# A mixed-heads attention and feed-forward kernel: second batch in float32, sums over partitions in two steps, the reciprocal behind the next maximum

## The chip, the core and the metric

The kernel runs on one core of one Trainium2 chip. The metric is the device time of one execution in microseconds (us); lower is better. The core has five engines that run their own instruction streams in order: PE (matrix products into PSUM), DVE (vector work), ACT (activation functions, copies with a scale), POOL (vector work on SBUF only) and SP, which issues nearly all transfers.

## What is computed

Two stages, joined by a reshape. Four batches, 12 heads, 448 positions, 64 features per head; then 1792 tokens of width 768 through a gated layer of width 2048.

```python
scale = 1.0 / np.sqrt(q.shape[-1])
scores = scale * np.matmul(q, k.transpose(0, 1, 3, 2))
scores = np.einsum('bhij,hg->bgij', scores, w_pre)      # mix the heads
scores = scores - np.max(scores, axis=-1, keepdims=True)
attn = np.exp(scores)
attn = attn / (np.sum(attn, axis=-1, keepdims=True) + 1e-09)
attn = np.einsum('bhij,hg->bgij', attn, w_post)         # mix the heads again
attn_out = np.matmul(attn, v)
...
h = x @ w_in                                            # x: attn_out as (1792, 768)
g = h * (1.0 / (1.0 + np.exp(-1.702 * h)))
out = g @ w_out
```

The mixing over heads is why a row of scores cannot stay inside one head: the kernel writes raw scores to DRAM (`sd`) and gathers them again with heads on partitions.

## The kernel before, in words

**Steps.** A batch's 448 query rows are cut in groups of 10 (45 groups, the last of 8). One group is one step of the main loop; `steps` lists all 180, so steps 0 to 44 are batch 0, 45 to 89 batch 1 and so on. With 12 heads a group fills 120 partitions.

In the loop turn i the code writes out, for the group i or its neighbours: `gather` for step i+4 (DMA of `r`), `mix(i+1)` on PE (the first head mixing, tile `mx`, two PSUM banks), then `peak(i)` on DVE (row maximum `nm`, read from `mx`), `expo(i)` on ACT (exponential `e` with its row sum `sm`) and, at its end, a short POOL instruction (`rs`, sum plus 1e-9). `inverse(i)` (line 304, a DVE reciprocal of `rs`) is the last thing of turn i. The next thing on DVE is `peak(i+1)`.

**Batch 0 is in float32.** `weigh_mix` (POOL) multiplies the small mixing matrix `wp` by the reciprocal, giving `wr`; `post_whole` (PE) forms the second mixing with four float32 products into `pp`, two turns after the group's own; `keep_whole` (ACT) copies `pp` to `p`. The context product (`context`, tile `av`) uses v and p in float32, and the scale that x gets is one number per batch (`xs`).

**Batches 1 to 3 split every operand in two float16 numbers.** `weigh` (POOL, `w` = e times `rs`), `upper` (ACT, `a1`) and `lower` (POOL, `a2` = w minus a1) split the weights; `post` (PE) does 12 float16 products per group, three turns after the group's own; `keep_upper` (ACT) and `keep_lower` (DVE, line 383) split the result. v is loaded twice, once for its size (`va`) and once to be split (`vb`, `vp`). q and k of batch 1 are float32 already before the change; those of batches 2 and 3 are split.

**Jobs.** The splitting of the two weight matrices (16 slices, `convert`), the loading and splitting of q, k and v, and the scales are jobs: each has an earliest turn, an engine, a cost and the jobs that it must follow. `run_jobs` is called once a turn, behind `peak` and `expo`, and starts what is due as long as its engine has tokens (4.3 a turn while nothing of the feed-forward runs, 5.2 after; jobs marked urgent don't ask). A slice of weights takes three parts: DVE decodes each with five instructions, ACT sums squares, then a sum over partitions and a scale follow, ACT writes the upper halves, DVE the lower halves (line 537), and SP stores them (`wd`).

**Sums over partitions.** `add_all` (lines 104 to 109) does such a sum in one job: a PE product with a matrix of ones into the last 16 columns of the newest `pp` bank, and directly behind it a DVE reduce of that product. There are 28 of them. DVE, which runs in order, stands at the reduce until PE has come to the product.

**The feed-forward part** is 384 quanta of six products each (`hidden`, 192, and `project`, 192). They begin when the x of a batch is complete; the loop then puts 2.15 quanta a turn behind the attention work. The first stands in turn 58. Behind the head mixing of step 179 PE still has 786 of these products left.

Of the kernel before, what the change touches and what calls it, by code (L numbers as in the profile page):

```python
# [19 lines left out]
B, H, S, D = 4, 12, 448, 64  # L20
DM, DFF = 768, 2048
# [17 lines left out]
def attention_then_feed_forward(ctx, tc, q, k, v, w_pre, w_post, w_in, w_out, out):  # L39
# [30 lines left out]
    wp = flow.tile([KG, H, GI], F32, name="wp", tag="th", bufs=2)  # L70
# [33 lines left out]
    def add_all(m, parts):  # L104
# [37 lines left out]
    def join(name, b):  # L142
        add_all(top_of(name, b), st["m" + name, b])

    def scale(name, b):
# [9 lines left out]
        if name == "v":  # L155
            nc.vector.tensor_scalar(
                ex[:, b:b + 1], e, e_wp, 2.0 ** -12, op0=ALU.mult, op1=ALU.mult
            )
            if b == 0:
                xs = st["xs"] = keep.tile([128, 1], F32, name="xs")  # L160
                nc.vector.reciprocal(xs, ex[:, 0:1])
# [61 lines left out]
    def scores(b, c, pr, tag=("gen", 3)):  # L223
# [5 lines left out]
        if b < 2:  # L229
# [59 lines left out]
    def expo(i):  # L289
# [6 lines left out]
        )  # L296
        rs = stat.tile([KG, 1], F32, name=f"rs_{i}", tag="rs")
        by = 2.0 ** -10 if steps[i][0] else 1.0
        nc.gpsimd.tensor_scalar(rs[:K], sm[:K], 1e-9, by, op0=ALU.add, op1=ALU.mult)  # L299
        row["e", i], row["rs", i] = e, rs  # L300
# [61 lines left out]
    def mixed_to(i):  # L362
# [3 lines left out]
        if off == 0:  # L366
            shape, kind = ([CP, NR, H, CI], F32) if b == 0 else ([CP, 2, NR, H, CI], F16)
            st["p", b, c] = mixed.tile(shape, kind, name=f"p_{b}_{c}", tag="p")
        p = st["p", b, c]
        if b == 0:  # L370
# [15 lines left out]
    def context(b, c, pr):  # L386
# [6 lines left out]
        if b == 0:  # L393
            for jc in range(NR):
                for d in range(2):
# [3 lines left out]
                        st["v", 0, h // w][:, h % w, jc * D:(jc + 1) * D],  # L399
                        st["p", 0, c][:, jc, h, :n],  # L400
# [21 lines left out]
    def x_upper(b, c, half, av):  # L422
        i0, n = chunk(b, c)
        by = st["xs"] if b == 0 else 2.0 ** -15
        nc.scalar.activation(x_of(b)[:, 0, 3 * half:3 * half + 3, i0:i0 + n], av, AF.Copy, scale=by)

    def x_lower(b, c, half, av):
        i0, n = chunk(b, c)
        x = x_of(b)[:, :, 3 * half:3 * half + 3, i0:i0 + n]
        by = st["xs"] if b == 0 else 2.0 ** -15  # L430
# [8 lines left out]

    def join_x(b):  # L440
        e = gs[:, b, 0:1]
        add_all(e, st["mx", b])
# [21 lines left out]
    def convert(kind, s, first):  # L464
# [46 lines left out]
        def join_w():  # L511
            t["n"] = stat.tile([128, 1], F32, name=f"{nm}_n", tag="wn")
            add_all(t["n"], t["m"])
# [45 lines left out]
        j = job(first, "D", 0.2, join_w, after=[(x, 1) for x in sizes])  # L559
# [173 lines left out]
    for b in range(1, B):  # L733
        z = GPB * b
        sizes = {}
        if b == 1:
            for i in range(THIRDS):
                for name in "kq":
                    job(z - 23 + 4 * i, None, 0, lambda name=name, i=i: load_whole(name, 1, i), urgent=True)
        for name, first, ready in (("k", z - 25, z - 17), ("q", z - 23, z - 17), ("v", z - 8, z + LAG + 7)):  # L740
            if b == 1 and name != "v":
                continue
# [6 lines left out]
            jn = job(0, "D", 0.2, lambda name=name, b=b: join(name, b), after=[(x, 1) for x in sq], urgent=True)  # L749
            sizes[name] = job(0, "D", 0.7, lambda name=name, b=b: scale(name, b), after=[jn], urgent=True)  # L750
# [6 lines left out]
        if b > 1:  # L757
            job(0, "D", 0.4, lambda b=b: mixing(b), after=[sizes["k"], sizes["q"]], urgent=True)
# [140 lines left out]
    j = job(1, "D", 0.2, lambda: join("v", 0), after=sq, urgent=True)  # L899
    job(1, "D", 0.9, lambda: scale("v", 0), after=[j], urgent=True)  # L900
# [51 lines left out]
    while quanta or i < N + LAG + 12:  # L952
# [15 lines left out]
        if GPB <= i - LAG - 1 < N:  # L968
            keep_upper(i - LAG - 1)
            spend("A", 0.55)  # L970
        if 0 <= i - 1 < GPB:
# [9 lines left out]
        if i < N:  # L981
            peak(i)
            spend("D", 0.62)
            expo(i)
            spend("A", 0.82)
# [7 lines left out]
        if GPB <= i - LAG < N:  # L993
# [6 lines left out]
        for b, c, pr in at_context.pop(i, []):  # L1000
# [7 lines left out]
            if c == NCH - 1 and pr == NPAIR - 1:  # L1008
                z = i
                a = job(z + 2, "D", 0.2, lambda b=b: join_x(b), urgent=True)  # L1010
# [4 lines left out]
                job(z + 3, "D", 0.9, finish, after=[a], urgent=True)  # L1015
# [4 lines left out]
        if GPB <= i - LAG - 1 < N:  # L1020
# [50 lines left out]
```

## Time and profile before

| | us |
|---|---|
| median of 3 runs (lowest, highest) | 1026.39 (1025.78, 1027.22) |
| the profiled execution | 1027.42 |
| its span, first to last instruction | 1025.7 |
| PE busy | 925.0 (90%) |
| DVE busy | 628.8 (61%) |
| ACT busy | 605.2 (59%) |
| POOL busy | 354.5 (35%) |
| mean granted PE clock | 0.961 |
| moved by DMA | 198.19 MB, 193 GB/s over the span |

PE is the busiest engine, but not evenly: its share is lower and its clock is below full speed in the first 45% of the span, and close to full afterwards. The transfers are the other way round: the busiest tenths of the DMA line are in the first fifth of the span. The views used below are the busy time by stage (a stage runs from the maximum of one step to that of another), the waits by stage, the groups of instructions, and the order of time for a few short stretches.

### The profile page before, as it was taken

What the parts mean: (1) busy time and instruction counts of PE and PEld (TensorE: products, weight loads), DVE (VectorE), ACT (ScalarE), POOL (GpSimd) and SP (SyncE); (2) the same over time, 40 slices, a digit from 0 to 9 for tenths busy, and PEclk for the clock granted to TensorE, in tenths of its full rate; (3) what the DMA queues carried; (4) which work ended last, traced back from release to release, by engine and by line L of the source; (5) the groups of instructions that cost most, each with busy time, mean ns of one, the idle gap of its engine ahead of it and who ended that gap; (6) DMA issues with size and microseconds to landing.
All of it is one profiled execution on the core that took longest, in us unless ns stands there. A gap on an engine that the chain in (4) does not pass through costs nothing.

```text
span 1025.7 us, 19868 instructions
## 1 busy us (share of the span) xinstructions
PE 925.0 (90%) x7344; PEld 542.4 (53%) x7344; DVE 628.8 (61%) x1389; ACT 605.2 (59%) x1380; POOL 354.5 (35%) x536
## 2 busy tenths in 40 slices
PE   5678878877899889999899999999899999999998
PEld 4345555544455444555455555656455666555554
DVE  5658786698976796554644575555645565443334
ACT  3666768677577676765657657656656564323332
POOL 0111111145433455343533454334534444001221
PEclk9888999888999998999999999999999999999999
DMA  8988979768557656654676647546654341234322
GB/s 301 289 275 313 332 267 323 259 197 245 190 198 244 232 187 181 192 172 131 202 225 207 202 150 234 166 130 179 212 164 146 108 148 64 93 123 151 118 93 85
DMA packets 66565, 198.19 MB, mean 193 GB/s; under 512 B 7668, under 2 KB 32372, under 8 KB 66468
## 3 DMA queue, kind: packets, MB, share of 16 engines
q1 hardware_dynamic: 66064, 196.83, 59.4%
q8 instruction: 58, 0.95, 0.4%
q14 instruction: 39, 0.32, 0.1%
q10 hardware_dynamic: 404, 0.09, 0.1%
HBM read 140.27 MB, written 56.62 MB: 192 GB/s over the span
## 4 chain that ended last, share of the span: by engine, by line
PE 62%; DVE 17%; ACT 8%; DMA 8%; issue 3%; POOL 1%; SPq 0%; ACTq 0%; DVEq 0%; POOLq 0%
PE po L627 19%; PE h L588 18%; PE mx L279 8%; PE av L408 4%; PE qk L243 3%; PE pp L356 2%; PE pp L358 2%; PE pp L357 2%; DVE w_p L537 2%; DMA sd<-sc 2%; ACT waste L96 2%; DVE w_f L504 2%; DMA w<-in_moe_w_out_dram 2%; DVE nm L286 2%; ACT e L293 1%
## 5 line engine op out<-in xcount | busy, mean ns | idle before, releaser
L627 PE MATMUL po<-g,wt 128*128 128x448 f16 x1152 | 243.8, 355 | 11.3 <-DVE th L609 6.8
L588 PE MATMUL h<-x,wt 128*128 128x448 f16 x1152 | 244.1, 356 | 3.9 <-ACT sc L253 2.9
L279 PE MATMUL mx<-r,wa 120*120 120x448 f32 x360 | 183.3, 592 | 40.0 <-ACT e L293 29.7
L343 POOL TENSOR_TENSOR a<-w,a 120x448 f16<-120x448 f32 x135 | 150.8, 1117 | 130.2 <-issue 71.5
L627 PEld LDWEIGHTS <-wt 128*128 128x128 f16 x1152 | 109.4, 99 | 130.0 <-issue 45.1
L588 PEld LDWEIGHTS <-wt 128*128 128x128 f16 x1152 | 109.2, 98 | 117.0 <-issue 31.2
L329 POOL TENSOR_SCALAR w<-e,rs 120x448 f32<-120x448 f32 x135 | 88.2, 653 | 227.3 <-DVE rs L304 217.8
L337 ACT ACTIVATE a<-e,rs 120x448 f16<-120x448 f32 x135 | 91.0, 674 | 106.1 <-DVE rs L304 106.1
L657 DVE SCALAR_TENSOR_TENSOR acc<-po,ct,acc 128x448 f32<-128x448 f32 x141 | 96.1, 682 | 74.3 <-PE po L627 72.2
L293 ACT ACTIVATE e<-mx,nm 120x448 f32<-120x448 f32 x180 | 113.6, 631 | 31.2 <-POOL wr L309 25.4
L609 DVE SCALAR_TENSOR_TENSOR th<-th,h 128x448 f32<-128x448 f32 x64 | 39.7, 620 | 137.8 <-ACT th L606 137.8
L606 ACT ACTIVATE th<-h,ct 128x448 f32<-128x448 f32 x64 | 40.5, 633 | 140.2 <-PE h L588 129.6
L253 ACT COPY sc<-qk 120x448 f32<-120x448 f32 (+1 forms) x186 | 89.6, 532 | 41.8 <-PE qk L233 28.9
L286 DVE TENSOR_REDUCE nm<-mx 120x1 f32<-120x448 f32 x180 | 108.9, 605 | 1.9 <-PE mx L279 1.9
L356 PE MATMUL pp<-wp,a 120*112 120x120 f16 x540 | 95.7, 220 | 14.8 <-DVE p L383 14.3
L279 PEld LDWEIGHTS mx<-r,wa 120*120 120x120 f32 x360 | 61.6, 193 | 83.9 <-ACT e L293 47.0
L299 POOL TENSOR_SCALAR rs<-sm 120x1 f32<-120x1 f32 x180 | 56.8, 315 | 115.8 <-ACT e L293 103.8
L358 PE MATMUL pp<-wp,a 120*112 120x120 f16 x540 | 95.1, 219 | 0.0
L357 PE MATMUL pp<-wp,a 120*112 120x120 f16 x540 | 94.9, 218 | 0.0
L383 DVE TENSOR_TENSOR p<-pp,p 112x480 f16<-112x480 f32 x135 | 87.2, 647 | 5.9 <-ACT p L379 5.9
L356 PEld LDWEIGHTS <-a 120*112 120x112 f16 x540 | 71.5, 132 | 26.9 <-DVE p L383 12.1
L357 PEld LDWEIGHTS <-a 120*112 120x112 f16 x540 | 71.8, 133 | 15.9 <-issue 9.5
(126 smaller groups left out, 1258.1 us busy)
## 6 DMA issues: line engine op xcount, KB each, us to landing
wt<-wd SPq DMA_DIRECT2D x64, 768.0 KB
r<-sd SPq DMA_DIRECT2D x176, 210.0 KB
sd<-sc SPq DMA_DIRECT2D x72, 420.0 KB
w<-in_moe_w_in_dram SPq DMA_DIRECT2D x24, 512.0 KB
w<-in_moe_w_out_dram SPq DMA_DIRECT2D x24, 512.0 KB
wd<-w_p SPq DMA_DIRECT2D x16, 768.0 KB
sd<-sc SPq DMA_DIRECT2D x24, 308.0 KB
out_dram<-acc SPq DMA_DIRECT2D x24, 224.0 KB
```

What stands on the lines that cost most here:

```text
L253: (nc.scalar.copy if engs[x] == "A" else nc.vector.tensor_copy)(t[:n, x, :], two[x][:n, :S])
L279: nc.tensor.matmul(mx[:K, :S], st["wa", b][:K, :K], row.pop(("r", i))[:K, :], start=True, stop=True)
L286: nc.vector.tensor_reduce(nm[:K], row["mx", i][:K, :S], axis=AX.X, op=ALU.max, negate=True)
L293: nc.scalar.activation(e[:K], row.pop(("mx", i))[:K, :S], AF.Exp, bias=row.pop(("nm", i))[:K, 0:1], scale=1.0, accum_out=sm[:K, 0:1],)
L337: nc.scalar.activation(a1[:K], row.pop(("e", i))[:K], AF.Copy, scale=row.pop(("rs", i))[:K, 0:1])
L343: nc.gpsimd.tensor_tensor(a2[:K], row.pop(("w", i))[:K], row["a1", i][:K], op=ALU.subtract)
L356: nc.tensor.matmul(o, a1[:K, js], wp1[:K, :, :n], start=True, stop=False)
L357: nc.tensor.matmul(o, a1[:K, js], wp2[:K, :, :n], start=False, stop=False)
L358: nc.tensor.matmul(o, a2[:K, js], wp1[:K, :, :n], start=False, stop=True)
L588: nc.tensor.matmul(h, w[:, i, c, fc * 128:(fc + 1) * 128], x[:, j, c, :], start=(n == 0), stop=(n == len(terms) - 1),)
L627: nc.tensor.matmul(po, w[:, j, fc, e * 128:(e + 1) * 128], g[:, i, fc, :], start=(n == 0), stop=(n == len(terms) - 1),)
L657: nc.vector.scalar_tensor_tensor(a, po, c, a, op0=ALU.mult, op1=ALU.add)
```

## The change

Three things are changed.

1. Batch 1 goes the way of batch 0: `WHOLE = 2` replaces the tests on batch 0. Its v is loaded once, whole; `weigh_mix`, `post_whole` and `keep_whole` take the place of `weigh`, `upper`, `lower`, `post`, `keep_upper` and `keep_lower`; the context product is float32; `xs` is kept for each of the two batches. The tile `wp` moves to a pool that lives on.
2. `add_all` is cut in two jobs: the PE product (`add_over`) in one turn, the DVE reduce (`add_along`) at the earliest in the next.
3. `inverse(i-1)` now stands in turn i, behind `peak(i)`; `expo(i)` comes ahead of `weigh_mix`/`weigh`, `upper` and `lower` of step i-1; the POOL instruction on the row sum becomes a function of its own (`shifted`) behind them.

```diff
+    def add_over(parts):
         p, n = parts.shape
         t = last_pp[-1][:, 512 - 16:512 - 16 + n]
         nc.tensor.matmul(t, ones[:p, :], parts, start=True, stop=True)
+        return t
+    def add_along(m, t):
         nc.vector.tensor_reduce(m, t, axis=AX.X, op=ALU.add)
+    def sum_jobs(first, m, parts, after):
+        t = {}
+        def over():
+            t["t"] = add_over(parts())
+        j = job(first, None, 0, over, after=after, urgent=True)
+        return job(first, "D", 0.2, lambda: add_along(m(), t["t"]), after=[j], urgent=True)
...
-        if b == 0:
+        if b < WHOLE:
             for jc in range(NR):
                 for d in range(2):
                     h = 2 * pr + d
...
-        j = job(first, "D", 0.2, join_w, after=[(x, 1) for x in sizes])
+        j = sum_jobs(first, total, lambda: t["m"], [(x, 1) for x in sizes])
...
-        if b == 1:
+        if b < WHOLE:
+            sq = []
             for i in range(THIRDS):
                 for name in "kq":
...
+                a = job(z + 7 + 2 * i, None, 0, lambda i=i, b=b: load_whole("v", b, i), urgent=True)
...
-        if 0 <= i - 2 < GPB:
+        if 0 <= i - 2 < WHOLE * GPB:
             post_whole(i - 2)
-        if 0 <= i - 3 < GPB:
+        if 0 <= i - 3 < WHOLE * GPB:
             keep_whole(i - 3)
...
+        if i < N:
+            peak(i)
+            spend("D", 0.62)
+        if 0 <= i - 1 < N:
+            inverse(i - 1)
+            spend("D", 0.15)
+        if i < N:
+            expo(i)
+            spend("A", 0.82)
...
-        if i < N:
-            inverse(i)
-            spend("D", 0.15)
```

How the instructions stand, at three places. In the rows, numbers behind a name tell one tile from the next, and the brackets name the engines or transfers that the instruction waits for; the new file's lines are numbered some 10 higher (286 becomes 297, 304 becomes 320, 109 becomes 113).

DVE in batch 0, around the sum of the third weight slice, before:

```order
L504 SCALAR_TENSOR_TENSOR w_2_f_1194<-w_2_64_2_1027,w_2_f_1194 128x512 [waits DVE_49]
L304 RECIPROCAL rs_1189<-rs_1189 120x1 [waits Pool_49]
L286 TENSOR_REDUCE nm_1214<-mx_1174 120x1 [waits PE_49]
L304 RECIPROCAL rs_1219<-rs_1219 120x1 [waits Pool_49]
L286 TENSOR_REDUCE nm_1250<-mx_1204 120x1 [waits PE_49]
L109 TENSOR_REDUCE w_2_n<-pp_1242 128x1 [waits PE_49]
L81 TENSOR_SCALAR w_2_n<-w_2_n 128x1 [waits DVE_49]
```

The same engine and place in the change:

```order
L447 SCALAR_TENSOR_TENSOR x_985<-av_0_3_1022,xs_590,x_985 128x3x120 [waits Activation_49]
L297 TENSOR_REDUCE nm_1166<-mx_1119 120x1 [waits PE_49]
L320 RECIPROCAL rs_1135<-rs_1135 120x1 [waits Pool_49]
L113 TENSOR_REDUCE w_2_n<-pp_1121 128x1 [waits PE_49,Activation_49]
L82 TENSOR_SCALAR w_2_n<-w_2_n 128x1 [waits DVE_49]
```

Each reciprocal now stands behind the maximum of the following step, and the reduce of the sum one turn later; it has taken on a wait for ACT, whose copy of the same `pp` bank is now written out ahead of it.

PE in batch 1, one turn before the change (of the 12 float16 products only the first three are shown; nine more of the same three lines follow):

```order
L279 MATMUL mx_2452<-r_2278,wa_255 120x448 [waits DMAHW0_49,Activation_49]
L356 LDWEIGHTS a_50_2342
L356 MATMUL pp_2475<-wp_84,a_50_2342 112x120 [waits DVE_49]
L357 LDWEIGHTS a_50_2342
L357 MATMUL pp_2475<-wp_85,a_50_2342 112x120
L358 LDWEIGHTS a_50_2344 [waits Pool_49]
L358 MATMUL pp_2475<-wp_84,a_50_2344 112x120
```

and in the change:

```order
L290 MATMUL mx_2340<-r_2214,wa_255 120x448 [waits DMAHW3_49,Activation_49]
L335 MATMUL pp_2342<-wr_2316,e_2269 112x120 [waits DVE_49,Pool_49]
L335 MATMUL pp_2342<-wr_2316,e_2269 112x120 x3
L244 MATMUL qk_2_1_0_2368<-kf_1_1137,qf_1_1139 120x448
L244 MATMUL qk_2_1_1_2369<-kf_1_1137,qf_1_1139 120x448
L413 MATMUL av_3_3_2286<-p_3_1750,vf_0_253 64x88 x8
L290 MATMUL mx_2386<-r_2256,wa_255 120x448 [waits DMAHW6_49,Activation_49]
```

Four float32 products stand where twelve float16 ones did, and they come one step earlier after the group's exponential. The feed-forward products, the scores and the head mixing stand in the same turns as before in all 180 steps.

ACT in batch 2, before (`a` is the upper half of the weights, `e` the next step's exponential):

```order
L379 CAST p_0_5575<-pp_5536 112x48x10
L337 ACTIVATE a_93_5579<-e_5523,rs_5526 120x448 [waits DVE_49,Activation_49]
L293 ACTIVATE e_5585,sm_5586<-mx_5512,nm_5583 120x448 [waits DVE_49,Pool_49]
L606 ACTIVATE th_0_5644<-h_0_5560,ct_5642 128x448 [waits DVE_49,PE_49]
L379 CAST p_0_5575<-pp_5597 112x48x10
```

and in the change:

```order
L395 CAST p_0_4698<-pp_4721 112x48x10
L304 ACTIVATE e_4763,sm_4764<-mx_4696,nm_4760 120x448 [waits DVE_49,Activation_49,Pool_49]
L353 ACTIVATE a_94_4768<-e_4703,rs_4712 120x448 [waits DVE_49]
L625 ACTIVATE g_4749<-th_0_4752,gs 128x448 [waits DVE_49]
```

The exponential of step i has moved ahead of the upper half of step i-1.

## Rows read from the trace of the kernel before

**Rows 1.** Busy time by stage: window, length; per engine busy us (instructions); PE clock, DMA share, GB/s
```profile
34.75:196.60 161.85, 130.14 (x804) 81.84 (x803) 119.11 (x310) 117.35 (x299) 30.15 (x90) 0.92 0.88 299
196.60:265.00 68.40, 50.83 (x372) 30.33 (x372) 56.35 (x119) 46.53 (x108) 30.27 (x41) 0.85 0.62 190
265.00:444.20 179.20, 162.23 (x1349) 92.66 (x1348) 129.21 (x274) 123.36 (x282) 76.70 (x100) 0.96 0.66 213
444.20:864.10 419.90, 405.22 (x3706) 242.02 (x3706) 239.02 (x512) 258.98 (x588) 188.93 (x272) 1.00 0.54 167
864.10:1025.70 161.60, 157.07 (x1042) 83.39 (x1036) 62.55 (x125) 49.68 (x85) 27.75 (x26) 1.00 0.32 111
```

**Rows 2.** Waits of DVE from 34.75 to 196.6: total us, times, longest
```profile
DVE rs L304 <- POOL rs L299: 17.1, 15, 3.3
DVE w_n L109 <- PE pp L108: 15.1, 8, 4.7
```

**Rows 3.** Waits of PE in the same window
```profile
PE mx L279 <- ACT e L293: 19.9, 15, 5.2
```

**Rows 4.** Order of time, DVE and then PE, 104 to 108: start, length
```profile
104.76 0.16 DVE L304 RECIPROCAL rs<-rs 120x1 f32<-120x1 f32 x1 [0.63 <-POOL rs L299]
107.16 0.16 DVE L109 TENSOR_REDUCE w_n<-pp 128x1 f32<-128x3 f32 x1 [1.71 <-PE pp L108]
...
105.16 1.01 PE L279 MATMUL mx<-r,wa 120*120 120x448 f32 x2
106.01 0.98 PE L319 MATMUL pp<-wr,e 120*112 120x120 f32 x8
106.83 0.29 PE L108 MATMUL pp<-w_m,ones 128*128 128x3 f32 x2
```

**Rows 5.** Transfers in the window 34.75 to 196.6: queue, packets, MB, share
```profile
q1 hardware_dynamic: 16232, 48.19, 87.4%
```

**Rows 6.** Order of time on PE: the float32 products of batch 0
```profile
92.63 1.04 PE L397 MATMUL av<-p,vf 112*64 112x120 f32 x16
93.60 1.01 PE L279 MATMUL mx<-r,wa 120*120 120x448 f32 x2
94.45 0.98 PE L319 MATMUL pp<-wr,e 120*112 120x120 f32 x8
95.36 1.02 PE L233 MATMUL qk<-kf,qf 64*120 64x448 f32 x4
```

**Rows 7.** Order of time on PE: the float16 products of batch 2
```profile
510.93 0.22 PE L356 MATMUL pp<-wp,a 120*112 120x120 f16 x1
...
511.56 1.30 PE L588 MATMUL h<-x,wt 128*128 128x448 f16 x6
...
519.87 0.82 PE L408 MATMUL av<-p,vp 112*64 112x120 f16 x24
520.62 1.31 PE L627 MATMUL po<-g,wt 128*128 128x448 f16 x6
```

**Rows 8.** Groups of instructions: busy us, mean ns, idle before and releaser
```profile
L343 POOL TENSOR_TENSOR a<-w,a 120x448 f16<-120x448 f32 x135 | 150.8, 1117 | 130.2 <-issue 71.5
L329 POOL TENSOR_SCALAR w<-e,rs 120x448 f32<-120x448 f32 x135 | 88.2, 653 | 227.3 <-DVE rs L304 217.8
L337 ACT ACTIVATE a<-e,rs 120x448 f16<-120x448 f32 x135 | 91.0, 674 | 106.1 <-DVE rs L304 106.1
L383 DVE TENSOR_TENSOR p<-pp,p 112x480 f16<-112x480 f32 x135 | 87.2, 647 | 5.9 <-ACT p L379 5.9
```

**Rows 9.** Waits of PE from 265 to 444.2
```profile
PE pp L356 <- DVE p L383: 7.8, 5, 3.3
PE pp L108 <- ACT p L379: 4.5, 4, 2.6
```

**Rows 10.** Waits of PE from 444.2 to 864.1
```profile
PE mx L279 <- ACT e L293: 3.1, 3, 1.1
```

**Rows 11.** The maxima of all steps: ns min/median/max, first and last start us
```profile
L286 DVE TENSOR_REDUCE nm<-mx x180: 596/605/625, 34.8 to 864.1; 120x1 f32<-120x448 f32 x176, 96x1 f32<-96x448 f32 x4
```

More of the change, by code (lines that the diff above doesn't have):

```diff
@@ L20 @@
 B, H, S, D = 4, 12, 448, 64
+WHOLE = 2
 DM, DFF = 768, 2048
@@ L69, in attention_then_feed_forward @@
     w_mix = keep.tile([KG, GI, H], F32, name="w_mix")
-    wp = flow.tile([KG, H, GI], F32, name="wp", tag="th", bufs=2)
+    wp = keep.tile([KG, H, GI], F32, name="wp")
     wp1 = keep.tile([KG, H, GI], F16, name="wp1")
@@ L158, in scale @@
             )
-            if b == 0:
-                xs = st["xs"] = keep.tile([128, 1], F32, name="xs")
-                nc.vector.reciprocal(xs, ex[:, 0:1])
+            if b < WHOLE:
+                xs = st["xs", b] = keep.tile([128, 1], F32, name=f"xs_{b}")
+                nc.vector.reciprocal(xs, ex[:, b:b + 1])
     def mixing(b):
@@ L296, in expo, with shifted @@
         )
+        row["e", i], row["sm", i] = e, sm
+    def shifted(i):
+        K = rows_of(steps[i][1])[1] * H
+        sm = row.pop(("sm", i))
         rs = stat.tile([KG, 1], F32, name=f"rs_{i}", tag="rs")
-        by = 2.0 ** -10 if steps[i][0] else 1.0
+        by = 1.0 if steps[i][0] < WHOLE else 2.0 ** -10
         nc.gpsimd.tensor_scalar(rs[:K], sm[:K], 1e-9, by, op0=ALU.add, op1=ALU.mult)
-        row["e", i], row["rs", i] = e, rs
+        row["rs", i] = rs
     def inverse(i):
@@ L735, in attention_then_feed_forward @@
         sizes = {}
-        if b == 1:
+        if b < WHOLE:
+            sq = []
             for i in range(THIRDS):
                 for name in "kq":
-                    job(z - 23 + 4 * i, None, 0, lambda name=name, i=i: load_whole(name, 1, i), urgent=True)
+                    job(z - 23 + 4 * i, None, 0, lambda name=name, i=i, b=b: load_whole(name, b, i), urgent=True)
+                a = job(z + 7 + 2 * i, None, 0, lambda i=i, b=b: load_whole("v", b, i), urgent=True)
+                sq.append(job(0, {"A": 1.6}, 0, lambda eng, i=i, b=b: squares("v", b, i, eng, 2), after=[(a, SENT)], urgent=True))
+            j = sum_jobs(0, lambda b=b: top_of("v", b), lambda b=b: st["mv", b], sq)
+            job(0, "D", 0.9, lambda b=b: scale("v", b), after=[(j, 0)], urgent=True)
+            continue
         for name, first, ready in (("k", z - 25, z - 17), ("q", z - 23, z - 17), ("v", z - 8, z + LAG + 7)):
-            if b == 1 and name != "v":
-                continue
             sq = []
@@ L748, in attention_then_feed_forward @@
                 a["stage"][1].append(sq[-1])
-            jn = job(0, "D", 0.2, lambda name=name, b=b: join(name, b), after=[(x, 1) for x in sq], urgent=True)
-            sizes[name] = job(0, "D", 0.7, lambda name=name, b=b: scale(name, b), after=[jn], urgent=True)
+            jn = sum_jobs(0, lambda name=name, b=b: top_of(name, b), lambda name=name, b=b: st["m" + name, b], sq)
+            sizes[name] = job(0, "D", 0.7, lambda name=name, b=b: scale(name, b), after=[(jn, 0)], urgent=True)
             for i in range(THIRDS):
@@ L756, in attention_then_feed_forward @@
                 a["stage"][1].extend([up, lo])
-        if b > 1:
-            job(0, "D", 0.4, lambda b=b: mixing(b), after=[sizes["k"], sizes["q"]], urgent=True)
+        job(0, "D", 0.4, lambda b=b: mixing(b), after=[sizes["k"], sizes["q"]], urgent=True)
     conv_done = {}
@@ L898, in attention_then_feed_forward @@
     sq = [job(1 + 2 * i, {"A": 1.6}, 0, lambda eng, i=i: squares("v", 0, i, eng, 2), urgent=True) for i in range(THIRDS)]
-    j = job(1, "D", 0.2, lambda: join("v", 0), after=sq, urgent=True)
-    job(1, "D", 0.9, lambda: scale("v", 0), after=[j], urgent=True)
+    j = sum_jobs(1, lambda: top_of("v", 0), lambda: st["mv", 0], sq)
+    job(1, "D", 0.9, lambda: scale("v", 0), after=[(j, 0)], urgent=True)
     at_scores = {}
```

42 lines of the change are left out of this document (16 added, 26 removed).

## The prediction, made before the change was run

> **What bounds the kernel now.** I read the busy time by stage first [rows 1]. The stages run from the maximum of one step to that of another (steps 0, 45, 59, 90, 179; first and last of them in [rows 11]): batch 0; the 14 steps in which batch 1 starts and no feed-forward product runs; the other 31 steps of batch 1, with feed-forward products; batches 2 and 3; and the feed-forward products that are left. The reader is to see that PE is the bound only in the last three. From 444.2 on it is busy 405.2 of 419.9 us and 157.1 of 161.6, at full clock. In batch 1's second part it is busy 162.2 of 179.2, clock 0.96. In the first two stages nothing is full: PE 130.1 of 161.85 and 50.8 of 68.4, at clocks of 0.92 and 0.85, DVE 119.1 and 56.4, ACT 117.4 and 46.5. There the order of the work, not its amount, sets the time.
>
> The waits say how. In batch 0 DVE stands 17.1 us for the POOL instruction on the row sum and 15.1 us for the PE product of a sum over partitions [rows 2], 32 of its 43 idle us. The next maximum queues behind both, the exponential behind the maximum, and PE waits 19.9 us for an exponential to free a bank of `mx` [rows 3].
>
> But not all of DVE's waiting costs time: [rows 4] show it standing 1.71 us for a sum while PE runs head mixing, second mixing and then the sum without a gap, work that had to be done anyway. And the transfers are close: their queue takes 87.4% of the 16 engines' time in this stage [rows 5].
>
> **The change, part by part.** The sum is made against the profiled execution, 1027.42 us (span 1025.7); it lies 1.0 us above the median of the runs, 1026.39.
>
> *Sums and reciprocal, batch 0 (161.85 us).* Both waits leave DVE's path: the reduce comes a turn later, when its product has long been done, and the maximum no longer stands behind the reciprocal. What is late next is PE, then the transfers. Bounds: nothing, if PE and the transfers cover all of it; at most what the transfers leave. They need 0.874 x 161.85 = 141.5 us; the three loads of v for its size (448 KB each) and a 512 KB part of the weights move out of this stage, 1.8 of 48.2 MB, so some 136 us, a gain of 26. PE's idle time, 31.7 us, allows no more than that either. I take a little under half of DVE's 32 us, 14, since the one row that shows both engines has the wait fully covered. At 148 us the transfers would be busy 92%. The two-step sums also put a slice of weights a turn or two later, six turns apart instead of five. Their fetches stay in the same turns; the last is stored in turn 91 and fetched in 95, so four turns cover it. If that cover went, the feed-forward products would stand for a landing transfer, and only one pair of slices is that close.
>
> *Batch 1 in float32, steps 45 to 58 (68.4 us).* Gone per group: on POOL 0.653 and 1.117, on ACT 0.674, on DVE 0.647 us [rows 8], and a split v. The steps become steps of batch 0. At that stage's old pace, 161.85/45 = 3.60 us, 14 steps take 50.4 us; at the pace forecast, 148/45 = 3.29, they take 46. The sizes of batch 1's v now fall here, and the first feed-forward products have to wait for the same x, so I take 51.4: a gain of 17. Bounds: 46 (a gain of 22), and half the gain, 60, if the start of the batch costs what it did. SP issues the new loads of v behind the last context products that read the old v; a wait there would queue the gathers behind it, but those run four steps ahead.
>
> *Batch 1 in float32, steps 59 to 89 (179.2 us).* Here the change adds work to the bound. Four float32 products of the second mixing take 95.36 - 94.45 = 0.91 us [rows 6], twelve float16 ones 511.56 - 510.93 = 0.63 [rows 7]: 0.28 more per group. A context product takes 93.60 - 92.63 = 0.97 [rows 6] against 520.62 - 519.87 = 0.75 [rows 7]: 0.22 more. For 31 groups and 16 products of full chunks that is 8.7 + 3.5 = 12.2 us on PE; over the whole of batch 1, 45 x 0.28 + 18 x 0.22 = 16.6 (six narrower products taken as even). Against it stand two waits of PE that lose their cause, 7.8 us for DVE's lower half and 4.5 for a sum [rows 9]: 12.3. So the two cancel. DVE and ACT lose 31 x 0.65 = 20 us each of work that PE could come to wait for, and a PE with fewer gaps may hold its clock: 4% of 162 us is 6.5. I take 5 us gained. Bounds: 12.2 lost if no wait goes; at best the work alone at full clock, 0.96 x 162.2 + 12.2 = 168, 11 gained.
>
> The Trainium skill (FP8 and Floating Point Precision, section TensorE Precision Notes) says that true float32 takes four passes through the array. By it four products are 16 passes where twelve float16 ones are 12, a third more, and 32 against 24 for the context; the rows have 44% and 29% more. By the rule the addition over batch 1 would be 45 x 0.21 + 18 x 0.25 = 14.0 us instead of 16.6. It speaks against this change, and the trace agrees that these products are dearer.
>
> *Batches 2 and 3 (419.9 us).* The exponential moves ahead of the upper half, the reciprocal behind the next maximum, so the halves come later by about one maximum, 0.6 us [rows 11]; the products that read them stand two turns further on, which hides it. PE idles only 14.7 us, and 3.1 of that is for an exponential [rows 10]. I take 2 gained; from 6 gained to 4 lost, were the halves late by 0.6 us in seven of the 90 steps.
>
> *The rest.* The prologue (34.75 us) and the last stage (161.6 us) keep their products. `wp` in another pool and the per-batch scale cost nothing: they add no instruction on an engine that is waited for.
>
> Sum: 14 + 17 + 5 + 2 = 38 us. 1027.4 - 38 = 989.4, and 1.0 less against the median: **988 us**.
>
> **The rivals.**
> *Covered* (1007 us, 0.20). DVE's waits in batch 0 are hidden by PE and the transfers; the stage keeps its time. For it: [rows 4] and the 87.4% of [rows 5]. Against it: PE's 19.9 us for exponentials. Then only the second stage gains, 18 at the old pace, with 1 elsewhere: 19 us.
> *All of it* (961 us, 0.18). Each stage reaches its best bound: 26 + 22 + 11 + 6 = 65 us. For it: three engines at 73 to 80% in batch 0. Against it: their loads are uneven from turn to turn, and there are only two `mx` banks between them.
> *The wait moves* (1009 us, 0.09). The reduce now waits for ACT's copy of its bank, as the order shows. ACT has 117.4/45 = 2.6 us of work a step; were it a step behind DVE each time, the eleven sums of the first two stages would cost 29 us of DVE, which eats the first stage's gain and the third's, and leaves 17.
> *PE pays for float32* (1043 us, 0.07), the slower side. The place is PE from the first float32 group of batch 1 to its last context product, the price 16.6 us. It decides if the first three stages together win back less than that: if batch 0 is covered, and the 17.6 idle us of PE in the second stage are set by feed-forward's wait for x rather than by the float16 chain. Against it: that stage is slower per step than batch 0 (4.89 against 3.60 us) with less PE work in it.
> The forecast has 0.46.
>
> **How the numbers follow.** Each rival is taken off the median. The range is to leave out no more than 0.2: from 964, which holds the better half of *all of it* out, to 1010, which takes in *covered* and *the wait moves*; left out are 0.09 and 0.07. A measurement of this kernel can tell about 0.2%, 2 us, from no change. Faster: the forecast, *covered*, *all of it*, and most of *the wait moves*, 0.90; slower 0.07; the rest, 0.03, within 0.2%.
>
> **What would show it.** In batch 0 DVE's waits for the row sum and for the sum's product should be nearly gone, and waits for `mx` from PE should appear; the stage should take 142 to 155 us with transfers above 90%. Steps 45 to 58 should run near 3.6 us each. In steps 59 to 89 PE should be busy over 95%, with no wait for a lower half before step 93. From step 90 to the end the time should be the same within 5 us. A wait of DVE for ACT in front of the reduce, or of PE for `r`, would prove me wrong in batch 0; a third stage longer than 182 us would mean that the float32 products cost more than the waits that they replace.

## The result, and where the time went

The changed kernel takes 994.50 us (median; 993.19 to 996.75) beside 1026.81 us of the kernel before on the same chip: a ratio of 0.9678, 95% interval 0.9642 to 0.9714. The prediction was 988 us, 964 to 1010. The profiled execution took 993.19 us, its span is 991.2.

The first view is the busy time by stage of the changed kernel, cut at the maxima of the same steps as [rows 1]: 0, 45, 59, 90, 179 and the end. Columns: window, length, then busy us of PE, PE's weight loads, DVE, ACT and POOL (number of instructions), PE's clock, share of the transfers, GB/s.

```profile
36.13:183.70 147.57, 127.75 (x806) 80.76 (x808) 111.00 (x281) 108.47 (x274) 35.61 (x89) 0.93 0.88 294
183.70:236.40 52.70, 44.85 (x327) 28.94 (x325) 37.46 (x102) 39.72 (x104) 11.46 (x28) 0.97 0.86 281
236.40:406.70 170.30, 165.41 (x1091) 98.76 (x1091) 113.19 (x274) 113.67 (x266) 45.06 (x73) 0.99 0.72 232
406.70:828.10 421.40, 406.10 (x3608) 241.26 (x3607) 240.26 (x506) 256.69 (x583) 186.17 (x270) 1.00 0.54 167
828.10:991.20 163.10, 158.37 (x1061) 84.50 (x1058) 63.03 (x126) 50.96 (x90) 29.03 (x29) 1.00 0.32 109
```

Against [rows 1]: steps 0 to 44 lost 14.3 us, steps 45 to 58 15.7, steps 59 to 89 8.9. Batches 2 and 3 grew by 1.5, the end by 1.5, and the prologue (34.75 to 36.13) by 1.4. In steps 59 to 89 PE now idles 4.9 us where it idled 17.0, at a clock of 0.99 where it had 0.96; its busy time rose by only 3.2 us although its products are dearer.

The waits of DVE in the first stage answer to [rows 2] (engine, line, what it waited for: total us, times, longest).

```profile
DVE nm L297 <- PE mx L290: 14.3, 10, 3.8
DVE w_n L113 <- ACT p L391: 11.7, 5, 3.2
DVE rs L320 <- POOL rs L315: 4.9, 7, 1.4
```

The reader is to see three things. The wait for the row sum went from 17.1 to 4.9. The wait ahead of the reduce of a sum (`w_n`) is still there, 11.7 us of 15.1; only its cause is new: ACT's copy of the same `pp` bank stands ahead of it. And a wait of the maximum for head mixing has appeared. Together they make 30.9 us where there were 32.2. All of DVE's idle time in the stage, the length less the busy time, fell from 42.7 to 36.6 us, and its work from 119.1 to 111.0; the two make the 14.3.

PE's wait for a free bank of `mx` [rows 3] went from 19.9 to 16.3. A wait that stands in no row so far fell by more, from 9.3 to 3.9: that of the context product for DVE's work on `x`, which reads an earlier context product. First the kernel before, then the change:

```profile
PE av L397 <- DVE x L431: 9.3, 3, 4.6
```

```profile
PE mx L290 <- ACT e L304: 16.3, 13, 2.7
PE av L413 <- DVE x L447: 3.9, 3, 1.7
```

The transfers [rows 5] moved 4.9 MB less at the same share:

```profile
q1 hardware_dynamic: 14925, 43.25, 87.9%
```

So the sum of the forecast was nearly met, stage by stage (38 us forecast, 34.5 between the two spans), but the waits that were to pay for the first stage had for the greater part only changed their names. The experiments ask which edit earned what.

### The profile page after: what moved, and what is told of

Same layout as the page of the kernel before. It is cut to its first block, busy times and chain, and to the rows that moved or that the text cites. A ratio compares the mean times of both kernels' runs of the same rounds, so it can differ in the third digit from the quotient of the medians.

```text
span 991.2 us, 18941 instructions
## 1 busy us (share of the span) xinstructions
PE 922.3 (93%) x6972; PEld 547.2 (55%) x6972; DVE 587.6 (59%) x1339; ACT 579.4 (58%) x1336; POOL 308.0 (31%) x495
## 4 chain that ended last, share of the span: by engine, by line
PE 61%; DVE 19%; ACT 8%; DMA 8%; issue 3%; POOL 0%; SPq 0%; ACTq 0%; DVEq 0%; POOLq 0%
PE po L639 19%; PE h L600 18%; PE mx L290 8%; PE av L424 3%; PE qk L254 2%; DVE w_f L510 2%; DVE nm L297 2%; PE pp L335 2%; DMA w<-in_moe_w_in_dram 2%; DVE w_p L549 2%; DVE w_f L516 2%; PE av L413 2%; DVE w_f L500 2%; DVE w_f L504 2%; PE pp L372 2%
## 5 line engine op out<-in xcount | busy, mean ns | idle before, releaser
L639 PE MATMUL po<-g,wt 128*128 128x448 f16 x1152 | 242.0, 353 | 11.7 <-DVE th L621 7.2
L600 PE MATMUL h<-x,wt 128*128 128x448 f16 x1152 | 239.5, 352 | 2.4 <-ACT sc L264 1.2
L359 POOL TENSOR_TENSOR a<-w,a 120x448 f16<-120x448 f32 (+1 forms) x90 | 96.0, 1067 | 103.7 <-issue 47.5
L335 PEld LDWEIGHTS pp<-wr,e 120*112 120x112 f32 x720 | 91.2, 184 | 40.0 <-issue 34.4
L325 POOL TENSOR_SCALAR wr<-wp,rs 120x120 f32<-120x120 f32 (+1 forms) x90 | 55.6, 618 | 159.2 <-DVE rs L320 112.8
L345 POOL TENSOR_SCALAR w<-e,rs 120x448 f32<-120x448 f32 (+1 forms) x90 | 64.5, 717 | 123.7 <-DVE rs L320 68.7
L290 PEld LDWEIGHTS mx<-r,wa 120*120 120x120 f32 x360 | 60.3, 188 | 71.3 <-ACT e L304 33.1
L335 PE MATMUL pp<-wr,e 120*112 120x120 f32 x720 | 92.6, 274 | 1.7 <-DVE gs L113 0.9
L315 POOL TENSOR_SCALAR rs<-sm 120x1 f32<-120x1 f32 x180 | 46.4, 258 | 150.9 <-ACT e L304 141.2
L666 POOL TENSOR_TENSOR acc<-acc,pt 128x448 f32<-128x448 f32 x32 | 36.9, 1156 | 135.7 <-ACT pt L663 135.3
L372 PE MATMUL pp<-wp,a 120*112 120x120 f16 x360 | 62.4, 217 | 3.8 <-DVE p L399 1.9
L353 ACT ACTIVATE a<-e,rs 120x448 f16<-120x448 f32 (+1 forms) x90 | 59.9, 666 | 4.9 <-DVE rs L320 4.8
L374 PE MATMUL pp<-wp,a 120*112 120x120 f16 x360 | 61.8, 216 | 0.0
```

What stands on the lines that cost most here:

```text
L290: nc.tensor.matmul(mx[:K, :S], st["wa", b][:K, :K], row.pop(("r", i))[:K, :], start=True, stop=True)
L335: nc.tensor.matmul(pp[:CP, jc * K:(jc + 1) * K], e[:K, jc * CP:(jc + 1) * CP], wr[:K, :, :n], start=True, stop=True,)
L345: nc.gpsimd.tensor_scalar(w[:K], e[:K], row["rs", i][:K, 0:1], 1.0, op0=ALU.mult, op1=ALU.mult)
L359: nc.gpsimd.tensor_tensor(a2[:K], row.pop(("w", i))[:K], row["a1", i][:K], op=ALU.subtract)
L372: nc.tensor.matmul(o, a1[:K, js], wp1[:K, :, :n], start=True, stop=False)
L374: nc.tensor.matmul(o, a2[:K, js], wp1[:K, :, :n], start=False, stop=True)
```

## Experiments

Each kernel is compared with the kernel before on its own chip; across chips the ratios are to be read, not the medians. First the edits apart, then what the two-step sums do, then the limits of the first stage.

### Float32 alone, and each edit taken out

Batch 1 back in float16, the two other edits kept (`f16_batch1`):

```diff
-WHOLE = 2
+WHOLE = 1
```

with the first loads and the splitting of v, and the float32 q and k, of batch 1 as in the kernel before.

> The changed kernel with batch 1 in float16 pairs again; sums in two steps and the reciprocal behind the next maximum stay. If the gain of the first stage comes from sums and reciprocal and that of steps 45 to 89 from float32: first stage near 148 us as in the changed kernel (147.6), steps 45 to 58 near 65 and 59 to 89 near 179, in all 994 + 12 + 9 = 1015 us. If instead the two later stages gained because DVE no longer waits, and float32 is only ballast there: they stay near 53 and 170 or fall, in all 985 to 997 us.

Sums in one step, the two other edits kept (`one_step_sums`):

```diff
-        j = job(first, None, 0, over, after=after, urgent=True)
-        return job(first, "D", 0.2, lambda: add_along(m(), t["t"]), after=[j], urgent=True)
+        def both():
+            over()
+            add_along(m(), t["t"])
+        return job(first, "D", 0.2, both, after=after, urgent=True)
```

> The changed kernel with product and reduce of a sum in one job again. Three theories on the first stage (161.85 us before, 147.6 after). If it gained because DVE no longer waits for the products, half of it, 7 us, comes back: 155 us there, 1002 in all. If it gained because the sums a turn later space the weight slices six turns apart instead of five and so move DVE work out of the stage: nearly all comes back, 160 there, 1007 in all (stores stand in turns 14, 19, 24 again here). If it is the reciprocal alone: 148 there, 995 in all.

The reciprocal back at the end of its own turn, and `expo` behind the upper half (`old_recip`):

```diff
-        if i < N:
-            peak(i)
-            spend("D", 0.62)
-        if 0 <= i - 1 < N:
-            inverse(i - 1)
-            spend("D", 0.15)
-        if i < N:
-            expo(i)
-            spend("A", 0.82)
...
         if i < N:
+            peak(i)
+            spend("D", 0.62)
+            expo(i)
+            spend("A", 0.82)
             shifted(i)
...
+        if i < N:
+            inverse(i)
+            spend("D", 0.15)
```

> The changed kernel with the reciprocal at the end of its own turn, ahead of the next maximum, and the exponential behind the halves of the step before, as in the kernel before; float32 and two-step sums stay. If the reciprocal's wait was on the path of the first stage: 155 us there and 1002 in all. If the slices' later turns made the gain: 148 there and 995 in all. For batches 2 and 3, 421.4 us after and 419.9 before: if the move costs there, this kernel is 1 to 3 us shorter in them.

Both of the last two at once, so that float32 is left alone (`only_f32`):

> Batch 1 in float32 alone: sums in one step and the reciprocal at the end of its own turn, as before. If the reciprocal is worth nothing in any company (the theory so far, from its undoing with the two-step sums in place), this is the kernel with one-step sums again: 1013 us, steps 0 to 44 in 160 us, steps 45 to 58 in 60, steps 59 to 89 in 168. The rival: the reciprocal is worth its place where DVE also stands for its own sums, which the two-step sums hide; then steps 0 to 44 take 165 us and more and the kernel 1018 to 1025.

| kernel | median us | ratio to before | steps 0–44 | 45–58 | 59–89 |
|---|---|---|---|---|---|
| before | 1026.8 | 1 | 161.8 | 68.5 | 179.2 |
| float32 alone | 1009.07 | 0.9811 (0.9793 to 0.9829) | 160.5 | 60.2 | 167.0 |
| float32 + reciprocal (`one_step_sums`) | 1012.88 | 0.9846 (0.9808 to 0.9885) | 160.6 | 60.3 | 167.5 |
| float32 + sums (`old_recip`) | 994.39 | 0.9657 (0.9626 to 0.9688) | 149.4 | 53.2 | 172.5 |
| sums + reciprocal (`f16_batch1`) | 1037.78 | 1.0073 (1.0047 to 1.0099) | 155.5 | 65.7 | 192.6 |
| all three (the change) | 994.50 | 0.9678 (0.9642 to 0.9714) | 147.6 | 52.7 | 170.3 |

The stages are those of one profiled execution each; a second execution of the change (`after_again`, below) has 146.6, 52.4 and 168.6. `f16_batch1` came out beyond both of its theories (1015 us, or 985 to 997). The other three came nearest to the theories by which the place of the weight slices makes the first stage and the reciprocal is worth nothing.

Read in pairs. **The reciprocal's move is worth nothing that can be measured**, with the two-step sums or without (rows 2 and 3, rows 4 and 6; their intervals overlap). Taken back, DVE's waits in the first stage are these:

```profile
DVE rs L320 <- POOL rs L315: 26.1, 19, 4.9
DVE w_n L113 <- ACT p L391: 8.0, 5, 2.3
DVE w_f L496 <- DMA w<-in_moe_w_in_dram: 1.2, 1, 1.2
DVE nm L297 <- PE mx L290: 0.2, 1, 0.2
```

The three waits, at the reciprocal, the sum and the maximum, make 34.3 us here and 30.9 in the change, where they are 4.9, 11.7 and 14.3: the move changes mostly the place at which DVE stands. **By the ratios the two-step sums are worth some 16 to 17 us on top of float32**, though they cost 3 to 5 us in the third stage. **Float32 is worth some 41 us with the two others, and some 19 us alone.** The two others without it make the kernel slower than before. So the parts don't add up: something in the two-step sums is bad for a float16 batch 1 and harmless to a float32 one.

### What do the two-step sums do: end a wait, or put work off?

A sum that ends a turn later puts the next slice of weights off as well: the slices follow each other in the same three tiles. Stored once in 5 turns before, they are stored once in 6 after. To see that alone, the kernel before with its slices begun six turns apart and nothing else (`late_slices`):

```diff
-            conv_done[kind, s] = convert(kind, s, n * 5 - NPAIR if n > 1 else EARLY + 10 * n)
+            conv_done[kind, s] = convert(kind, s, n * 6 - 8 if n > 1 else EARLY + 10 * n)
```

> The kernel before with one number changed: a slice of weights may start every six turns instead of every five (stores in turns 14, 20, 26, 32, 38, 45 as against 14, 19, 24, 29, 34, 39), so that as much DVE work leaves the first stage as in the changed kernel; nothing else is touched. If the first stage gained by the moved work: 148 to 152 us there, and in all 1015 to 1018, less what the work costs later. If it gained by the waits: 161 there, 1026 in all.

Measured: 1036.4 us, 1.0083 (1.0054 to 1.0111). Steps 0 to 44 took 158.0 us, between the two theories: they gained 3.9, and steps 45 to 58 5.3, but steps 59 to 89 took 191.9, nearly the 192.6 of `f16_batch1`. The two third stages by busy time, `f16_batch1` first (columns as above):

```profile
258.11:450.70 192.59, 162.25 (x1346) 91.44 (x1345) 142.21 (x294) 127.89 (x294) 89.66 (x105) 0.96 0.64 204
```

```profile
257.21:449.08 191.87, 164.78 (x1349) 93.24 (x1348) 147.40 (x304) 128.16 (x294) 83.54 (x104) 0.95 0.65 206
```

DVE has 142 and 147 us of work there instead of 129.2 [rows 1]: the put-off slices. PE idles 30 and 27 us. Of these, the largest waits in `late_slices` are for what DVE and ACT leave in the `pp` banks, the pair of [rows 9], longer now:

```profile
PE pp L356 <- DVE p L383: 9.5, 8, 2.0
PE pp L108 <- ACT p L379: 5.7, 3, 4.6
```

This is what float32 buys: without the halves, DVE has 113.2 us of work in that stage of the change with the same late slices, and PE's wait for a lower half doesn't exist. That answers why the parts don't add up. One difference stays open: the first stage of `f16_batch1` is 7.9 us longer than that of the change, though batch 1 does no more there than load v for its size. PE waits 8.1 us for `x` there and 2.1 for a gather, where the change has 3.9 and none; what makes `x` late isn't shown.

The same question with float32 in place: sums in one step, slices six turns apart (`one_step_late`, the two edits above together).

> The change with sums in one step, but with the weight slices begun six turns apart (n*6-8 in place of n*5-6), so that the slices lie where the two-step sums put them. Theory 1, the sums gain by putting slices off: steps 0 to 44 take 147 to 151 us, steps 45 to 58 near 53, the kernel 993 to 999 us, although DVE stands some 15 us for the product of the sum. Theory 2, they gain because DVE no longer stands for that product: steps 0 to 44 stay at 157 to 160 us, the kernel at 1006 to 1012 us.

Measured: 1004.01 us, 0.9763 (0.9736 to 0.9790), between the two theories. Its first stage, and DVE's waits in it:

```profile
35.90:189.40 153.50, 127.90 (x800) 81.39 (x799) 109.81 (x277) 109.19 (x276) 33.81 (x89) 0.93 0.83 279
```

```profile
DVE w_n L113 <- PE pp L109: 18.5, 7, 6.3
DVE nm L299 <- PE mx L292: 11.0, 8, 3.4
DVE rs L322 <- POOL rs L317: 8.2, 12, 2.1
```

and the same stage of `one_step_sums`, whose slices are five turns apart:

```profile
35.63:196.21 160.58, 127.80 (x802) 81.51 (x801) 119.41 (x302) 113.25 (x287) 36.94 (x89) 0.93 0.88 295
```

DVE's busy time falls by 9.6 us and the stage by 7.1; DVE's idle time rises a little (41.2 to 43.7). From `one_step_late` to the change DVE's busy time stays (109.8 and 111.0), its idle time falls from 43.7 to 36.6, and the stage by 5.9. So both theories hold, each for a part of the 13 us.

PE shows where the time was lost. Its busy time is 127.8, 127.9 and 127.8 us in the three kernels, so the 13 us are its idle time. Its waits in `one_step_sums`, then in `one_step_late`:

```profile
PE mx L292 <- ACT e L306: 14.8, 16, 2.4
PE mx L292 <- DMA r<-sd: 9.3, 4, 3.4
PE av L415 <- DVE x L449: 8.4, 3, 3.6
```

```profile
PE mx L292 <- ACT e L306: 12.9, 15, 1.9
PE av L415 <- DVE x L449: 7.7, 3, 3.2
PE mx L292 <- DMA r<-sd: 4.9, 2, 2.8
```

The head mixing stands for an exponential or a gather 24.1 us, 17.8 and, in the change, 16.3 (all for exponentials); the context product stands for `x` 8.4, 7.7 and 3.9. The wait for the exponential alone doesn't fall. The three stages:

| | 0–44 | 45–58 | 59–89 | span |
|---|---|---|---|---|
| `one_step_sums` | 160.6 | 60.3 | 167.5 | 1008.0 |
| slices later: `one_step_late` | −7.1 | −7.7 | +8.4 | 1003.4 |
| the sum's reduce a turn later too: the change | −5.9 | +0.1 | −5.6 | 991.2 |

In these single executions, putting the slices off mostly moves time from one stage to another, 4.6 us net, and the two-step sum itself gives 12.2. The ratios, which take in all executions (0.9846, 0.9763, 0.9678), give the two about the same: 8.5 and 8.7 us, each to some 5 us.

### The wait that is left ahead of the reduce

If standing there costs time, the 11.7 us that are left do too. The reduce at the head of the next turn, ahead of ACT's copy of the bank (`early_reduce`):

```diff
             t["t"] = add_over(parts())
+            pending.append(lambda: add_along(m(), t["t"]))
...
-        return job(first, "D", 0.2, lambda: add_along(m(), t["t"]), after=[j], urgent=True)
+        return job(first, "D", 0.2, lambda: None, after=[j], urgent=True)
...
         if i + 1 < N:
             mix(i + 1)
+        while pending:
+            pending.pop(0)()
         if 0 <= i - 2 < WHOLE * GPB:
             post_whole(i - 2)
```

> The change with the reduce of a sum at the head of the turn after its product, ahead of ACT's copy of the same bank, so that it no longer waits for that copy; the product itself stays in its turn. If the 11.7 us that DVE waits for ACT ahead of the reduce in steps 0 to 44 cost time, that wait falls under 5 us, the stage shrinks by 4 to 8 us from 147.6 and the kernel comes to 986 to 991 us. If ACT, which now has to wait for the reduce, takes the same time back, or the transfers set the stage, the stage stays within 2 us and the kernel at 993 to 996 us.

And a middle place, behind the next maximum and reciprocal but still ahead of ACT's copy (`mid_reduce`): the flush of `pending` stands behind `inverse(i - 1)`, and `keep_whole` and `keep_upper` behind that.

> The change with the reduce of a sum behind the next turn's maximum and reciprocal, but ahead of ACT's copy of the same bank: between the change (behind that copy) and the reduce at the head of the turn, where DVE stood 9.8 us for PE's product in steps 0 to 44. If DVE's path still counts, the wait for the product falls under 5 us and the kernel comes to 984 to 988 us. If the transfers set steps 0 to 44, that stage stays within 2 us of 144.5 and the kernel at 987 to 992 us.

They were compared with the change on one chip:

> The changed kernel once more, beside the two kernels that move the reduce, so that they are compared on one chip: 992 to 997 us. If its lead over them was an effect of the chip, it comes within 2 us of them.

> The kernel with the reduce at the head of the next turn once more, beside the changed kernel: 987 to 991 us, 4 to 6 us under it, if the wait for ACT's copy costs time; within 2 us of it if not.

| | median us (lowest to highest) | ratio to before | 0–44 | 45–58 | 59–89 | 90–178 |
|---|---|---|---|---|---|---|
| `after_again` | 995.23 (992.11 to 996.24) | 0.9670 (0.9647 to 0.9694) | 146.6 | 52.4 | 168.6 | 423.3 |
| `early_again` | 990.54 (985.64 to 993.83) | 0.9633 (0.9604 to 0.9662) | 144.2 | 52.1 | 168.3 | 423.7 |
| `mid_reduce` | 991.37 (989.84 to 997.53) | 0.9654 (0.9627 to 0.9680) | 142.3 | 52.3 | 169.2 | 426.2 |

`early_reduce` itself had 989.12 us and 0.9621 (0.9593 to 0.9648). The medians of this kernel lie 4.7 us (on one chip) and 5.4 us under the change's; the intervals still touch, so some half a per cent is likely, not certain. It is the fastest kernel measured here. `mid_reduce` comes close to it, but did not reach the 984 to 988 us of its first theory. DVE's waits in its first stage, and in that of `mid_reduce`:

```profile
DVE nm L299 <- PE mx L292: 9.8, 13, 1.4
DVE w_n L114 <- PE pp L110: 9.8, 4, 4.8
DVE rs L322 <- POOL rs L317: 8.6, 11, 1.7
```

```profile
DVE nm L299 <- PE mx L292: 14.1, 13, 4.0
DVE rs L322 <- POOL rs L317: 11.9, 13, 2.4
```

With the reduce at the head of the turn DVE stands for PE again, 9.8 us (8.4 in `early_again`), where it stood 11.7 for ACT (9.4 in `after_again`). In the middle place the wait for a sum is gone from the list altogether, and the stage falls to 142.3 us; but the other waits have grown, 26.0 us together where the change had 19.2, so that more than half of those 11.7 us were stood elsewhere. Whether the rest shortened the stage is asked at the end of the next section. Behind step 90 `mid_reduce` was 3 us slower than the other two; why, these runs don't show.

### Do the transfers set the first stage?

They are busy 88% of it. Two runs, one with more of them and one with fewer. More: each gather of batch 0 made again a turn later, into the same tile (`extra_gather`):

```diff
             gather(i + AHEAD)
+            if i < GPB and i + AHEAD - 1 < GPB:
+                again(i + AHEAD - 1)
```

> The change with each gather of batch 0 from step 4 on made twice, into the same tile and with the same data, the second one a turn later: some 40 times 210 KB more, 8.6 MB on top of 43.3 in steps 0 to 44. If the transfers set that stage, it grows by most of their time, 20 to 26 us, to 168 to 174 us at a share over 90%. If latency between engines sets it, with transfers only beside it, it stays within 4 us of 147.6 while the share rises above 95%, or grows by under 10.

Measured: the first stage took 187.6 us, 40 more, beyond both theories, at no higher share (87.3% of the queue). SP's own waits say why:

```profile
SPq L289 <- DMA r<-sd: 80.4, 29, 5.9
```

The second gather of a tile has to wait for the first to land, on SP, and all other transfers queue behind it; PE stands 31.9 us for gathers there, none in the change. The run measured a blocked queue, not the transfers; it says nothing on the question. Fewer: the gathers of odd steps left out (`half_gathers`):

```diff
+        if b == 0 and i % 2:
+            row["r", i] = last_r[0]
+            return
-        t = flow.tile([KG, S], F32, name=f"r_{i}", tag="r", bufs=4)
+        t = last_r[0] = flow.tile([KG, S], F32, name=f"r_{i}", tag="r", bufs=4)
```

> The change, but the 22 gathers of the odd steps of batch 0 are left out: their head mixing reads the tile of the step before, so these steps compute on the wrong scores, with all their other instructions in place. 4.6 MB less in steps 0 to 44. If the transfers set that stage at about 293 GB/s, it loses up to 4.6/0.293 = 16 us, down to 132 to 138 us, where PE (127.8 us busy at a clock of 0.93) comes next; the other stages stay. If the order of the engines sets it, it stays within 4 us of 147.6 and the share of the transfers falls to 0.79.

```profile
36.59:180.50 143.91, 123.81 (x808) 78.90 (x808) 111.65 (x282) 107.70 (x274) 35.12 (x89) 0.98 0.81 271
```

4.4 MB less, and the stage is 3.7 us shorter, not 16; the share falls to 0.81. `mid_reduce` runs the stage in 142.3 us with all its transfers, at a share of 0.91. So at 0.88 the transfers don't set it. PE's waits agree: in the change it stands for exponentials and for `x` in this stage, never for a gather. What is left is the order between the engines.

The stage is also PE's busy time plus its idle time. The rows of the kernels not shown so far, `after_again`, `early_again` and `mid_reduce`:

```profile
36.13:182.71 146.58, 126.04 (x806) 80.10 (x808) 111.25 (x281) 108.46 (x274) 35.12 (x89) 0.95 0.89 299
```

```profile
35.87:180.02 144.15, 124.77 (x806) 79.53 (x808) 110.66 (x281) 108.61 (x274) 35.91 (x89) 0.95 0.90 302
```

```profile
36.24:178.54 142.30, 122.74 (x808) 78.33 (x808) 111.09 (x282) 107.92 (x274) 36.02 (x89) 0.98 0.91 306
```

| steps 0–44 | PE busy us | PE idle us | PE clock |
|---|---|---|---|
| before | 130.1 | 31.7 | 0.92 |
| `one_step_sums` | 127.8 | 32.8 | 0.93 |
| `one_step_late` | 127.9 | 25.6 | 0.93 |
| the change | 127.8 | 19.8 | 0.93 |
| `after_again` | 126.0 | 20.5 | 0.95 |
| `early_again` | 124.8 | 19.4 | 0.95 |
| `mid_reduce` | 122.7 | 19.6 | 0.98 |
| `half_gathers` | 123.8 | 20.1 | 0.98 |

From the kernel before to the change it is the idle time that falls, 11.9 of the 14.3 us. Among the last five it is the same within 1.2 us. What differs there is the busy time of the same products, at another granted clock (a mean over stretches at 2.4 and at 1.2 GHz), and by 1.7 us even between two executions of the change. So neither the wait ahead of the reduce nor half of the gathers, taken away, shortened PE's standing in this stage by more than about a microsecond. Whether the higher clock comes of these edits or by chance, these runs don't show.

## Why the prediction was right, and where its steps were not

**Steps 0 to 44** (forecast 14, measured 14.3): the right size by a wrong working. The step "Both waits leave DVE's path" failed. The wait for the sum stayed at 11.7 of 15.1 us, now for ACT, which is the prediction's own sign of being wrong there; the wait for the row sum came back as one for `mx`; the moved reciprocal earned nothing. The path behind these waits failed too: PE's wait for an exponential, at its end, fell by only 3.6 us, and its wait for `x`, which the prediction doesn't have, by 5.4. That the term still came out at 14 is luck. What earned the 14 us was the part that the prediction named and gave no price, "a slice of weights a turn or two later, six turns apart instead of five": some 7 us of DVE's work pushed into later stages, and some 6 of idle time saved by the two-step sum, as the pair through `one_step_late` shows. The doubt drawn from [rows 4], that DVE's wait was covered by work due anyway, was right for the reciprocal. What was late next was not the transfers, as the prediction had it; "transfers above 90%" did not come (0.88, with 4.9 MB gone from the stage and not 1.8), and with 4.4 MB fewer still PE's idle time did not move.

**Steps 45 to 58** (forecast 17, measured 15.7; 3.76 us a step against "near 3.6"). The size holds, but float32 brought 8.2 of it alone (`only_f32`, 60.2 us). That is the half gain that the prediction had for its bound, "if the start of the batch costs what it did". The rest came with the late slices: `one_step_late` has 52.6. PE's clock, which the prediction did not price in this stage, has a part in both: from the kernel before to the change PE's idle time fell from 17.6 to 7.9 us, and its busy time from 50.8 to 44.9 at a clock of 0.97 in place of 0.85.

**Steps 59 to 89** (forecast 5, measured 8.9). This mechanism was right: PE's wait for a lower half and its wait for a sum are gone from the list of its waits, PE is busy 97% and its clock is 0.99. Alone float32 gains 12.2 us (167.0), more than the bound of 11, since PE's busy time hardly grew: 163.0 us at a clock of 1.00 against 162.2 at 0.96. At full clock that is some 7 us more (163.0 less 0.96 x 162.2, an estimate), where the prediction added 12.2 for the dearer products. The prediction's cover for the late slices ("four turns cover it") looked only at their fetches. Their work was not priced: it costs 12.7 us in float16 (`late_slices`) and 8.4 in float32 (`one_step_late`), of which the two-step sums return 5.6.

**Batches 2 and 3** (forecast 2 gained, measured 1.5 lost) lie within the bounds given. Steps 108 to 134 take 138.1 to 138.9 us in the kernels with one-step sums and 138.7 to 141.0 in those with two-step ones; but all of steps 90 to 178 take 419.9 to 423.7 us in the first and 420.7 to 426.2 in the second, so the 1.5 us can't be put down to the sums. **The end** is 1.0 to 1.6 us longer in every kernel with the moved reciprocal than in those without; step 179's maximum, from which it is counted, then no longer stands behind a reciprocal, and steps 135 to 178 of the change are 0.6 us shorter.

**The rivals.** *The wait moves* was right on the wait and wrong on its price: DVE stood for ACT at five of the seven weight sums of the first stage, 11.7 us in all, and the kernels that avoid it are some 2 to 6 us shorter by the ratios, not 29. *Covered* was right for the reciprocal alone. *All of it* would have needed 26 us in the first stage; even `mid_reduce` has 19.5 there. *PE pays for float32* fell: in the third stage PE's busy time rose by 3.2 us.

## What to carry to other kernels

When waits on an engine are to be removed, add up all its waits and its busy time in that stage before and after: a wait that comes back under another name has earned nothing, and a shorter busy time means that work has gone to another stage, where it must be priced. A stage can also get shorter because the products in it ran at a higher clock; PE's busy and idle time, taken apart, show which it was. An edit that delays one link of a chain of jobs shifts the whole chain; whether that helps depends on the stage that receives the work, so such edits are judged together with those that make room there. And when a small reduce reads a bank that another engine also reads, look at which of the two is written out first: the later one waits for both. Here that wait was 11.7 us and worth about half a per cent at most.

## What was not expected of the hardware

The POOL instruction that forms `wr` (120x120, the same in both kernels) took 366 ns on average before, in the window from 36 to 444 us, and takes 618 in the change:

```profile
L309 POOL TENSOR_SCALAR wr<-wp,rs 120x120 f32<-120x120 f32 (+1 forms) x45 | 16.5, 366 | 66.3 <-DVE rs L304 60.3 <-PE pp L319 3.1 <-PE mx L279 1.8
```

```profile
L325 POOL TENSOR_SCALAR wr<-wp,rs 120x120 f32<-120x120 f32 (+1 forms) x90 | 55.6, 618 | 159.2 <-DVE rs L320 112.8 <-PE mx L290 9.6 <-DVE w_n L113 9.3
```

In steps 0 to 44 its mean is 559 ns in the change and 392 with the reciprocal back in its old place, so it goes with that move. The order of time of POOL and DVE in the change shows a long one and a short one (start, length):

```profile
104.92 0.65 POOL L325 TENSOR_SCALAR wr<-wp,rs 120x120 f32<-120x120 f32 x1 [1.01 <-DVE rs L320]
...
107.08 0.39 POOL L325 TENSOR_SCALAR wr<-wp,rs 120x120 f32<-120x120 f32 x1 [1.24 <-PE pp L335]
```

```profile
104.66 0.67 DVE L516 SCALAR_TENSOR_TENSOR w_f<-w,w_f 128x512 int32<-128x512 int32 x1
...
106.83 0.41 DVE L496 TENSOR_SCALAR w_f<-w 128x512 int32<-128x512 int32 x1
```

The long one starts 0.26 us behind a DVE instruction that reads two tensors of SBUF, and ends 0.24 us after it; the short one lies beside DVE instructions that read one. The other steps agree: of the 44 `wr` instructions in steps 0 to 44 of the change, 17 lie beside a DVE instruction with two tensors of SBUF that started before them or within 3 ns, and took 652 to 1295 ns; the other 27 took 364 to 388. In the kernel before none took over 367 ns; ten have such a DVE instruction beside them too, but it started some 0.27 us or more behind them. No wait of PE for `wr` stands in the list of that stage. With the reciprocal behind the maximum, DVE goes straight on to decode weights while `wr` is formed; before, the next thing was a maximum, which reads PSUM. The Trainium skill (SBUF — State Buffer, section SBUF: two separate sides) says that DVE and GpSimd share one pair of ports, and that an instruction of DVE with two inputs from SBUF, if it starts first, holds the pair alone until it ends, against a GpSimd instruction that reads SBUF. These rows agree with it; POOL's spans are rough, and no run here takes the DVE instruction away.
